# A transformer block pair on one core: one product shared by two projection tiles, and a later chunk's transposes placed in an earlier wait

## The chip, the cores and the metric

The kernel runs on one core of one Trainium2 chip. The metric is device time in microseconds (us). A time is the median of three runs. A profile is one further execution, with every instruction's start and length. Below, PE is TensorE (matmuls; its weight loads are PEld), DVE is VectorE, ACT is ScalarE, POOL is GpSimd and SP is SyncE, whose queue issues nearly all transfers.

## The reference

Two layers, each of multi-query attention (16 heads of width 28, one key and one value head) and a gated feed-forward, on 2048 rows of width 448, with the same weights in both layers.

```python
def _A_ref(x, wq, wk, wv, wo):
    q = (x @ wq).reshape(B, S, H, Dh).transpose(0, 2, 1, 3)
    k = x @ wk
    v = x @ wv
    scores = jnp.einsum("bhqd,bkd->bhqk", q, k) * (Dh ** -0.5)
    o = jnp.einsum("bhqk,bkd->bhqd", _softmax(scores), v)
    return o.transpose(0, 2, 1, 3).reshape(B, S, H * Dh) @ wo

def _B_ref(x, w_gate, w_up, w_down):
    return (_silu(x @ w_gate) * (x @ w_up)) @ w_down

x = x + _A_ref(_layernorm(x), ...)
x = x + _B_ref(_layernorm(x), ...)
x = x + _A_ref(_layernorm(x), ...)
x = x + _B_ref(_layernorm(x), ...)
```

Everything is float32. The kernel splits each operand of a product into a rounded high part and a remainder (h and l, float32r) and adds three products: high by high, high by low, low by high.

## The kernel before

The 2048 rows are cut into four chunks of 512. The order in which the code is written is the order on each engine; no scheduler moves instructions. An engine works through its own instructions in that order and waits where one of them has to.

**Projections.** For each chunk there are four tiles of 128 columns, 16 products per layer. They are called q0 to q15 here, in the order of `Attention.order`; q0 to q3 belong to chunk 0, q12 to q15 to chunk 3. A tile holds 112 columns of queries and 16 of keys or values. `project()` runs one tile: first what `plan[n, 0]` names, then the transposes of a chunk that is due (`turned`, by `flip`), then the product (`q`), then what `plan[n, 1]` and `when[n]` name. `q` takes a PSUM bank, runs `product_T`, and then evacuates: ScalarE casts the queries (L538), ScalarE copies the tile to a buffer named `stage` (L539), SP issues its store to DRAM (`qd`, L540, and for two tiles of a chunk the keys to `kt`, L543), and for the other two VectorE transposes the value columns (L546) and GpSimd places them (L549). In layer 0 there are three `stage` buffers, in layer 1 two, so there a copy waits until the stores of the tile before last have landed.

**The inner dimension** is 448: three slices of 128 and one of 64. For the last slice `xh[:, 3]` holds the high part in its lower 64 partitions and the remainder in its upper 64, and the weights stand in both halves. So one product of 128 rows gives two of the three terms. The third takes one more product, with the weights' low part `wl`, whose upper half adds the low part times the remainder, a term that the other slices leave out. That makes 11 products a tile:

```python
        for k in range(3):
            seq += [(a_h[k], xh[:, k, :]), (a_h[k], xl[:, k, :]), (a_l[k], xh[:, k, :])]
        seq += [(a_h[3], xh[:, 3, :]), (a_l[3], xh[:, 3, :])]
```

**The feed-forward** already works by half rows: products of 64 rows on partitions 0 to 63 and 64 to 127 are issued alternately by `side_by_side` (L332) into two banks and run at the same time. For it a third tile `xd` holds the last slice's high part in partitions 64 to 127.

**Chunks of layer 1.** Chunks 0 to 2 are transposed by VectorE into DRAM at the end of the feed-forward of layer 0, loaded back by SP (`load`, L934 to L937, into the buffers `qstack`), and split into `xh` and `xl` by `halved`: ScalarE casts (L292, L296), VectorE subtracts (L293, L302). Chunk 3 is transposed by TensorE (`flip`, L248, 16 transposes) from the normalised tile `xn`; ScalarE casts from PSUM (L254, L258) and VectorE subtracts (L255, L264). For chunk 2 the load is issued after q4 (`plan[4, 1]`), and the splitting, called `parts`, stands ahead of q7 (`plan[7, 0]`). SP has one queue: after the load of chunk 2 come a load of keys (`wrk`, L398), four of queries (`qraw`, L421) and then the stores of q5. Each transfer of the queue also takes one of eight completion counters (DMAHW0 to DMAHW7), in turn, and waits until the transfer that had it before has landed.

Of the kernel before, what the change touches and what calls it, by code (L numbers as in the profile page):

```python
# [9 lines left out]
F32R = mybir.dt.float32r  # L10
# [5 lines left out]
P = 128  # L16
# [7 lines left out]
NC = S // 512  # L24
# [31 lines left out]
def forward(  # L56
# [14 lines left out]
    nc = tc.nc  # L71
# [13 lines left out]
    xpool = ctx.enter_context(tc.tile_pool(name="xpool", bufs=1))  # L85
# [4 lines left out]
    wide = [ALL]  # L90
# [20 lines left out]
    def bank(cands, hold=False):  # L111

        for _ in cands:
            turn[cands] = (turn.get(cands, -1) + 1) % len(cands)
            b = cands[turn[cands]]
            if b not in live:
                if hold:
                    live.add(b)
                return b, banks[b]
        raise AssertionError("no bank")  # L120
# [82 lines left out]
    def xtile(pool, again=None):  # L203

        return (
            pool.tile([P, 4, 512], F32R, name="xh"),
            pool.tile([P, 3, 512], F32R, name="xl"),
            again,
        )
# [33 lines left out]
    def flip(got, tiles, ks=range(4), place=None):  # L243

        for k in ks:
            pt = place if place is not None else bank(wide[-1])[1]
            for t in range(4):
                nc.tensor.transpose(pt[:, P * t : P * t + P], got["x"][:, t, P * k : P * k + P], ident)  # L248
            flipped(tiles, k, pt, nc.vector.tensor_copy if place is not None else nc.scalar.copy)
# [16 lines left out]
    def turn_tile(got, tb, t):  # L266

        nc.vector.transpose(tb[:, :, 32 * t : 32 * t + 32], got["x"][:, t, 0:D].rearrange("p (b w) -> p b w", w=32))
# [7 lines left out]
    def natural(po, squares):  # L276

        if not squares:
            return po
        return po.rearrange("p (g t w) -> p t g w", g=4, w=32)  # L280

    def in_order(a, squares):

        return a.rearrange("p (t g w) -> p t g w", g=4, w=32) if squares else a
# [19 lines left out]
    def product_T(po, a_h, a_l, tiles):  # L304

        xh, xl = tiles[:2]
        seq = []
# [3 lines that stand above are left out]
        for i, (a, b) in enumerate(seq):  # L311
            nc.tensor.matmul(po, a, b, start=(i == 0), stop=(i == len(seq) - 1))  # L312
# [14 lines left out]
    def side_by_side(lower, upper):  # L327

        assert len(lower) == len(upper)
        for two in zip(lower, upper):  # L330
            for po, (a, b), start, stop in two:
                nc.tensor.matmul(po, a, b, start=start, stop=stop, skip_group_check=True)  # L332
# [10 lines left out]
    class Attention:  # L343
# [152 lines left out]
        def project(self):  # L496

            c, m = self.order[self.seen]
            for f in self.plan.get((self.seen, 0), ()):
                f()  # L500
            late = self.layer == 0 and self.seen == 3
            turned = [self.order[n][0] for n in (self.seen, self.seen + 1) if n % 4 == 0 and n < len(self.order)]
            for o in turned if not late else ():
                self.turned(o)
            self.q(c, m)
            for o in turned if late else ():
                self.turned(o)
            for f in self.plan.get((self.seen, 1), []) + self.when.pop(self.seen, []):
                f()
            self.seen += 1  # L510

        def turned(self, c):
            if c in self.norms:
                flip(self.norms.pop(c), self.X[c])

        def q(self, c, m):
            cs = slice(512 * c, 512 * c + 512)
            sq = c in self.squares
            held, po = bank((3, 4, 5) if self.seen > len(self.order) - 4 else wide[-1], True)
            ms = slice(P * m, P * m + P)  # L520
            wh, wl = self.w
            product_T(po, [wh[:, k, ms] for k in range(4)], [wl[:, k, ms] for k in range(4)], self.X[c])
            if not full and self.seen in (6, 10, 14):
                self.maxima(self.seen // 4 - 1)()
            live.remove(held)
            if c not in self.qd:
                self.qd[c] = dram.tile([D, 512], F32, name=f"qd{self.layer}_{c}")
            if self.layer and c == NC - 1:
                if "xn" not in self.spare:
                    self.spare["xn"] = pers.tile([P, 4, 512], F32, name="xn")  # L530
                raw = self.spare["xn"][:, self.seen % 4, :]
            else:
                raw = self.pool.tile([P, 512], F32, name="stage")
            if not full:
                if self.seen % 2 == 0:
                    self.two = wpool.tile([P, 2, 512], F32R, tag="wgh", name="q2", bufs=FG + 1)
                self.hi[c, m] = self.two[0:112, self.seen % 2, :]
                nc.scalar.copy(in_order(self.hi[c, m], sq), natural(po[0:112, :], sq))  # L538
            nc.scalar.copy(in_order(raw, sq), natural(po, sq))  # L539
            nc.sync.dma_start(self.qd[c][112 * m : 112 * m + 112, :], raw[0:112, :])  # L540
            d0, n = 16 * (m % 2), 12 if m % 2 else 16
            if m > 1:
                nc.sync.dma_start(self.kt[c][d0 : d0 + n, :], raw[112 : 112 + n, :])  # L543
                return
            vt = wpool.tile([P, 512], F32R, tag="wgl", name="vt", bufs=FG + 1).bitcast(F32)[96:128, :]
            nc.vector.transpose(vt, po[96:128, :])  # L546
            vt = vt.rearrange("p (u t d) -> p u t d" if sq else "p (t u d) -> p u t d", t=4, u=4)
            for u in range(4):
                nc.gpsimd.tensor_copy(  # L549
                    vsb[32 * u : 32 * u + 32, 4 * c : 4 * c + 4, d0 : d0 + n], vt[:, u, :, 16 : 16 + n]  # L550
                )
# [285 lines left out]
    class FeedForward:  # L837
# [61 lines left out]
        def hand_over(self, c):  # L899

            a = self.nxt
            fs, got = norm_steps(c, twice=c == NC - 1)
            for f in fs[:5]:
                f()
            a.pool = self.stage

            if c == NC - 1:

                def ready():
                    for f in fs[5:]:  # L910
                        f()
                    a.norms[c] = got

                a.X[c] = xtile(self.xbp)
                a.plan[5, 1] = [ready]
                return
            to = dram.tile([D, 512], F32, name=f"xt1_{c}")
            raw = [q.bitcast(F32)[:, z, :] for q in qts[1:] for z in range(2)]

            def turn():  # L920
                for f in fs[5:]:
                    f()
                pool = (xpool, self.x1p, self.xbp)
                tb = pool[min(c + 1, 2)].tile([P, 4, 512], F32R, name="xh").bitcast(F32)
                tb = tb.rearrange("p a (b n) -> p (a b) n", n=P)[:, 0 : D // 32, :]
                for t in range(4):
                    turn_tile(got, tb, t)
                send(tb, to)
                a.X[c] = xtile(pool[c])
                if c < 2:  # L930
                    load()

            def load():
                nc.sync.dma_start(qts[1].bitcast(F32), to[0:256, :].rearrange("(k p) n -> p k n", p=P))  # L934
                nc.sync.dma_start(raw[2], to[256:384, :])
                for half in (slice(0, 64), slice(64, 128)):
                    nc.sync.dma_start(raw[3][half, :], to[384:448, :])  # L937

            def parts():
                halved(a.X[c], raw, range(4), nc.scalar.copy, nc.vector.tensor_tensor)  # L940

            self.soon.append([1, turn])
            if c == 2:
                a.plan[4, 1] = [load]
                a.plan[7, 0] = [parts]
                return
            self.soon.append([3, parts])
            self.soon.append([4 - c, lambda: [a.project() for _ in range(2 - c)]])
# [128 lines left out]
    xb = ExitStack()  # L1077
    at = Attention(0)
    at.pool = xb.enter_context(tc.tile_pool(name="stage_", bufs=3))
    xbp = xb.enter_context(tc.tile_pool(name="xb0", bufs=3))  # L1080
# [16 lines left out]
    for c in (1, 2, 3):  # L1097
        load_x(c, nc.sync)
    at.below(nc.sync)
    at.X = {c: xtile(xpool if c == 0 else xbp) for c in range(NC)}  # L1100
    at.turned(0)
    nc.gpsimd.memset(vsb, 0.0)
    nc.gpsimd.memset(vsb[:, :, DH : DH + 1], 1.0)
# [15 lines left out]
    for layer in range(2):  # L1119
# [3 lines left out]
        xb = ExitStack()  # L1123
        at.scores(ff, xb)
        ff.rest(xb)
        at = ff.nxt
# [28 lines left out]
```

## Time and profile before

| | us |
|---|---|
| median of three runs | 1962.71 (1962.13 to 1963.45) |
| the profiled execution | 1962.25 |
| its span, first instruction to last | 1960.4 |
| projections of layer 0, from q0 to the first score | 12.0 to 63.7 |
| attention of layer 0 | 63.7 to 556 |
| feed-forward of layer 0 | 556 to 971 |
| projections of layer 1 among the last units of the feed-forward | 971.9 to 1032.9 |
| attention, then feed-forward of layer 1 | 1032.9 to 1526, to 1960.4 |

A row of a timeline gives the start, the length, the engine, the source line, the operation, output and inputs by name, the shape, and a count where equal rows were merged; in brackets stands the idle time before it and what ended it. Matmuls are pipelined, so one of 0.39 us length is followed by the next long before that time is over: what one costs is read from start to start. A product of 128 rows has "128\*128" and one of half rows "64\*128" in its row. On the SP queue (SPq) a row is the issue of a transfer, not the transfer.

### The profile page before, as it was taken

What the parts mean: (1) busy time and instruction counts of PE and PEld (TensorE: products, weight loads), DVE (VectorE), ACT (ScalarE), POOL (GpSimd) and SP (SyncE); (2) the same over time, 40 slices, a digit from 0 to 9 for tenths busy, and PEclk for the clock granted to TensorE, in tenths of its full rate; (3) what the DMA queues carried; (4) which work ended last, traced back from release to release, by engine and by line L of the source; (5) the groups of instructions that cost most, each with busy time, mean ns of one, the idle gap of its engine ahead of it and who ended that gap; (6) DMA issues with size and microseconds to landing.
All of it is one profiled execution on the core that took longest, in us unless ns stands there. A gap on an engine that the chain in (4) does not pass through costs nothing.

```text
span 1960.4 us, 44004 instructions
## 1 busy us (share of the span) xinstructions
PE 1943.3 (99%) x18469; PEld 1325.5 (68%) x18469; DVE 968.3 (49%) x1638; ACT 1264.1 (64%) x1888; POOL 553.6 (28%) x593
## 2 busy tenths in 40 slices
PE   9999999999999999999999999999999999999998
PEld 7544545445468999999974445454454799988886
DVE  6656575665743223223666565657656433223223
ACT  4899898998943333333349998989989333333332
POOL 4213123132214333333341221121231332323320
PEclk9999999999999999999999999999999999999999
DMA  5111011121130011110251110110211200011102
GB/s 166 55 36 29 21 40 40 29 53 43 26 87 20 17 32 32 32 29 19 67 156 34 37 30 22 50 28 24 67 40 32 71 28 21 17 32 32 32 2 77
DMA packets 100643, 83.61 MB, mean 43 GB/s; under 512 B 25080, under 2 KB 81656, under 8 KB 100440
## 3 DMA queue, kind: packets, MB, share of 16 engines
q1 hardware_dynamic: 98888, 79.55, 14.7%
q8 instruction: 145, 2.38, 0.5%
q10 hardware_dynamic: 1552, 1.20, 0.2%
q14 instruction: 58, 0.48, 0.1%
HBM read 57.38 MB, written 21.50 MB: 40 GB/s over the span
## 4 chain that ended last, share of the span: by engine, by line
PE 87%; ACT 9%; DMA 1%; DVE 1%; issue 1%; POOL 0%; SPq 0%; ACTq 0%; POOLq 0%; DVEq 0%
PE bank L332 40%; PE bank L688 20%; PE bank L633 14%; ACT pt L655 6%; PE three L633 5%; PE bank L312 4%; ACT pair L656 2%; PE three L612 2%; PE bank L612 1%; PE three L621 0%; PE bank L438 0%; DMA kt<-stage 0%; DMA xd<-xh 0%; DMA wr<-in_A_wq_dram 0%; DVE vt L546 0%
## 5 line engine op out<-in xcount | busy, mean ns | idle before, releaser
L655 ACT ACTIVATE pt<-three 128x1536 f32<-128x1536 f32 x512 | 723.0, 1484 | 52.9 <-PE three L633 52.9
L688 PE MATMUL bank<-pt,vsb 128*32 128x512 f32 x3072 | 490.8, 599 | 0.0
L688 PE MATMUL bank<-pair,vsb 128*32 128x512 f32 x1024 | 487.5, 598 | 0.6 <-ACT pair L656 0.6
L633 PE MATMUL bank<-qstack,keys 32*128 32x512 f32 x1536 | 473.1, 425 | 0.0
L332 PE MATMUL bank<-xh,wgh 64*128 64x512 f32 x1728 | 450.7, 389 | 0.0
L633 PE MATMUL three<-qstack,keys 32*128 32x512 f32 x4608 | 428.7, 408 | 0.5 <-ACT stage L539 0.3
L633 PEld LDWEIGHTS bank<-qstack,keys 32*128 32x128 f32 x1536 | 243.5, 183 | 250.0 <-issue 124.9
L654 DVE COPY pair<-bank 128x512 f32<-128x512 f32 x512 | 354.0, 691 | 95.2 <-PE bank L633 57.4
L332 PE MATMUL bank<-xh,wgl 64*128 64x512 f32 x1404 | 371.7, 391 | 0.0
L332 PE MATMUL bank<-xl,wgh 64*128 64x512 f32 x1296 | 338.1, 390 | 0.0
L332 PE MATMUL bank<-wdh,h 64*128 64x448 f32 x1792 | 334.3, 364 | 1.1 <-ACT h L1008 0.8
L1007 DVE TENSOR_TENSOR sg<-bank,sg 128x512 f32<-128x512 f32 x112 | 77.4, 691 | 502.5 <-ACT sg L1006 500.3
L656 ACT ACTIVATE pair<-pair 128x1024 f32<-128x1024 f32 x256 | 281.5, 1100 | 0.0
L332 PEld LDWEIGHTS bank<-xh,wgh 64*128 64x128 f32 x1728 | 266.3, 185 | 16.7 <-issue 1.3
L633 PEld LDWEIGHTS three<-qstack,keys 32*128 32x128 f32 x4608 | 261.5, 183 | 13.9 <-DVE xres L604 1.5
L885 POOL TENSOR_TENSOR xres<-stage,xres 128x448 f32<-128x448 f32 x108 | 127.3, 1197 | 502.5 <-ACT stage L884 502.3
L688 PEld LDWEIGHTS bank<-pt,vsb 128*32 128x32 f32 x3072 | 101.9, 109 | 246.0 <-issue 153.1
L332 PEld LDWEIGHTS bank<-wdh,h 64*128 64x128 f32 x1792 | 247.5, 184 | 14.8 <-issue 2.0
L697 DVE TENSOR_TENSOR o<-bank,o 128x512 f32<-128x512 f32 x224 | 154.9, 691 | 203.8 <-PE bank L688 203.8
L339 ACT COPY seen<-bank 128x1 f32<-128x1 f32 x664 | 81.9, 163 | 254.3 <-PE bank L332 251.2
L332 PEld LDWEIGHTS bank<-xh,wgl 64*128 64x128 f32 x1404 | 219.2, 184 | 13.8
L332 PE MATMUL bank<-wdl,h 64*128 64x448 f32 x896 | 222.2, 367 | 0.0
(145 smaller groups left out, 2095.7 us busy)
## 6 DMA issues: line engine op xcount, KB each, us to landing
o<-rd SPq DMA_DIRECT2D x32, 256.0 KB
qraw<-qd SPq DMA_DIRECT2D x128, 56.0 KB
qd<-stage SPq DMA_DIRECT2D x28, 224.0 KB
wdr<-in_B_w_down_dram SPq DMA_DIRECT2D x28, 224.0 KB
xt<-tb SPq DMA_DIRECT2D x24, 224.0 KB
wr<-in_B_w_gate_dram SPq DMA_DIRECT2D x28, 192.0 KB
wr<-in_B_w_up_dram SPq DMA_DIRECT2D x28, 192.0 KB
xn<-xt SPq DMA_DIRECT2D x6, 768.0 KB
```

Source lines behind the costliest of these rows:

```text
L312: nc.tensor.matmul(po, a, b, start=(i == 0), stop=(i == len(seq) - 1))
L332: nc.tensor.matmul(po, a, b, start=start, stop=stop, skip_group_check=True)
L339: nc.scalar.copy(seen[:, i : i + 1], po[:, 0:1])
L612: nc.tensor.matmul(po[:, 0:D], a[:, g, P * t : P * t + P], b[:, g, :], start=False, stop=(g == NG - 1 and z == 2), skip_group_check=True,)
L633: nc.tensor.matmul(three[:, j, :] if j < 3 else one, k[js, kp, ks], q[js, part, :], start=(z == 0), stop=(z == 2), tile_position=(32 * j, 0),)
L654: copies.append(nc.vector.tensor_copy(pt1, one))
L655: es.append(nc.scalar.activation(pt, threes[y], AF.Exp, scale=SCALE))
L656: es.append(nc.scalar.activation(pair, pair, AF.Exp, scale=SCALE))
L688: nc.tensor.matmul(to[32 * j : 32 * j + 32, :], vsb[:, n % NT, :], pts[n][j], start=(y == 0), stop=(y == 1), skip_group_check=True,)
L697: f = nc.vector.tensor_tensor(accs[i][:, 0, :], to, accs[i][:, 0, :], ALU.add)
L885: nc.gpsimd.tensor_tensor(r, s, r, ALU.add)
L1007: nc.vector.tensor_tensor(in_order(sg, sq), natural(pg[1], sq), in_order(sg, sq), ALU.mult)
```

## The change

Two tiles of a chunk share the eleventh product. The first of a pair (q0, q2, ...) runs ten products of 128 rows, and then two of 64 rows side by side: on the lower half its own third term of the last slice, and on the upper half the third term of the second tile, which opens the second tile's bank; it reads `xd`. The second tile then runs its ten products into that bank. This holds for all chunks but chunk 0 of layer 0, which has no `xd`. For it the chunks get an `xd` tile, and the last slice is cast in two halves (L299 and L300 in `halved`, L261 and L262 in `flipped`, lines of the changed kernel), where it was one cast. In layer 1 the transposes of chunk 3 move from q11 to q8, and chunk 2's `parts` from ahead of q7 to ahead of q8.

```diff
@@ project
             turned = [self.order[n][0] for n in (self.seen, self.seen + 1) if n % 4 == 0 and n < len(self.order)]
+            if self.layer and self.seen == 8:
+                turned = [NC - 1]
             for o in turned if not late else ():
                 self.turned(o)
@@ Attention
+        def pair(self, po):
+
+            c, m = self.order[self.seen]
+            xh, xl, xd = self.X[c]
+            wh, wl = self.w
+            ms = slice(P * m, P * m + P)
+            a_h, a_l = [wh[:, k, ms] for k in range(4)], [wl[:, k, ms] for k in range(4)]
+            seq = []
+            for k in range(3):
+                seq += [(a_h[k], xh[:, k, :]), (a_h[k], xl[:, k, :]), (a_l[k], xh[:, k, :])]
+            seq.append((a_h[3], xh[:, 3, :]))
+            if self.seen % 2:
+                for i, (a, b) in enumerate(seq):
+                    nc.tensor.matmul(po, a, b, start=False, stop=(i == 9), skip_group_check=True)
+                return
+            for i, (a, b) in enumerate(seq):
+                nc.tensor.matmul(po, a, b, start=(i == 0), stop=False, skip_group_check=True)
+            m2 = self.order[self.seen + 1][1]
+            self.next = self.own_bank(1)
+            side_by_side(
+                [(po, (wl[0:64, 3, ms], xh[0:64, 3, :]), False, True)],
+                [(self.next[1], (wl[64:128, 3, P * m2 : P * m2 + P], xd[64:128, :]), True, False)],
+            )
+
+        def own_bank(self, ahead):
+
+            return bank((3, 4, 5) if self.seen + ahead > len(self.order) - 4 else wide[-1], True)
@@ q
-            held, po = bank((3, 4, 5) if self.seen > len(self.order) - 4 else wide[-1], True)
...
-            product_T(po, [wh[:, k, ms] for k in range(4)], [wl[:, k, ms] for k in range(4)], self.X[c])
+            if self.X[c][2] is None:
+                held, po = self.own_bank(0)
+                product_T(po, [wh[:, k, ms] for k in range(4)], [wl[:, k, ms] for k in range(4)], self.X[c])
+            else:
+                held, po = self.next if self.seen % 2 else self.own_bank(0)
+                self.pair(po)
@@ hand_over (c == NC - 1)
-                a.X[c] = xtile(self.xbp)
+                a.X[c] = xtile(self.xbp, self.xd[c])
@@ hand_over (turn)
-                a.X[c] = xtile(pool[c])
+                a.X[c] = xtile(pool[c], self.xd[c])
@@ hand_over (c == 2)
-                a.plan[7, 0] = [parts]
+                a.plan[8, 0] = [parts]
@@ forward
-    at.X = {c: xtile(xpool if c == 0 else xbp) for c in range(NC)}
+    xdp = xb.enter_context(tc.tile_pool(name="xd_", bufs=1))
+    at.X = {c: xtile(xbp, xdp.tile([P, 512], F32R, name=f"xd_{c}")) for c in range(1, NC)}
+    at.X[0] = xtile(xpool)
```

TensorE's order in layer 0, at the border between q4 and q5 (the first pair), before. The bank's name ends in a number of its own; `wh` and `wl` are the weights' two parts:

```order
L312 MATMUL bank_83<-xl,wh 128x512
L312 MATMUL bank_83<-xh,wl 128x512
L312 MATMUL bank_83<-xh,wh 128x512
L312 MATMUL bank_83<-xh,wl 128x512
L312 MATMUL bank_84<-xh,wh 128x512
L312 MATMUL bank_84<-xl,wh 128x512
L312 MATMUL bank_84<-xh,wl 128x512
```

The same border in the changed kernel:

```order
L530 MATMUL bank_83<-xl,wh 128x512
L530 MATMUL bank_83<-xh,wl 128x512
L530 MATMUL bank_83<-xh,wh 128x512
L332 MATMUL bank_83<-xh,wl 128x512
L332 MATMUL bank_84<-xd_221,wl 128x512
L527 MATMUL bank_84<-xh,wh 128x512
L527 MATMUL bank_84<-xl,wh 128x512
L527 MATMUL bank_84<-xh,wl 128x512
```

The last product of q4 has become two of half rows (L332), the second into q5's bank, and at q5's end the same product is gone.

ScalarE's order in layer 1 at q7 and the splitting of chunk 2, before. `stage_11645` is q6's buffer, `stage_11677` q7's; the brackets name what an instruction waits for:

```order
L539 COPY stage_11645<-bank2_6437 128x512 [waits DMAHW1_49,DMAHW0_49,Activation_49]
L292 CAST xh_11492<-qstack1_101 128x512 [waits DMAHW2_49]
L292 CAST xh_11492<-qstack1_101 128x512
L292 CAST xh_11492<-qstack2_102 128x512 [waits DMAHW3_49]
L296 CAST xh_11492<-qstack2_102 128x512 [waits DMAHW5_49,DMAHW4_49]
L538 CAST q2_11646<-bank3_6438 112x512 [waits PE_49]
L539 COPY stage_11677<-bank3_6438 128x512 [waits DMAHW4_49,DMAHW3_49,Activation_49]
```

And in the changed kernel, where `stage_11658` is q6's and `stage_11681` q7's:

```order
L573 COPY stage_11658<-bank2_6447 128x512 [waits DMAHW1_49,DMAHW0_49,Activation_49]
L572 CAST q2_11659<-bank3_6448 112x512 [waits PE_49]
L573 COPY stage_11681<-bank3_6448 128x512 [waits DMAHW4_49,DMAHW3_49,Activation_49]
L292 CAST xh_11505<-qstack1_101 128x512 [waits DMAHW2_49]
L292 CAST xh_11505<-qstack1_101 128x512
L292 CAST xh_11505<-qstack2_102 128x512
L299 CAST xd2_6632<-qstack2_102 64x512 [waits DMAHW5_49]
L300 CAST xh_11505<-qstack2_102 64x512
L254 CAST xh_11575<-bank4_6449 128x512 [waits DMAHW6_49,DVE_49,PE_49]
```

q7's cast and copy now stand ahead of chunk 2's casts, the last cast is two, and behind them come the casts of chunk 3 out of PSUM. VectorE's order in the changed kernel at the same place (before, the L293 and L302 rows stood between the two value transposes, then L546):

```order
L580 STREAM_TRANSPOSE vt_11663<-bank2_6447 32x512 [waits Activation_49]
L580 STREAM_TRANSPOSE vt_11685<-bank3_6448 32x512 [waits PE_49,Activation_49]
L293 TENSOR_TENSOR xl_11506<-qstack1_101,xh_11505 128x512 [waits DMAHW2_49,Activation_49]
L293 TENSOR_TENSOR xl_11506<-qstack1_101,xh_11505 128x512 [waits Activation_49]
L293 TENSOR_TENSOR xl_11506<-qstack2_102,xh_11505 128x512 [waits DMAHW3_49,Activation_49]
L302 TENSOR_TENSOR xh_11505<-qstack2_102,xd2_6632 64x512 [waits DMAHW5_49,Activation_49]
L255 TENSOR_TENSOR xl_11576<-bank4_6449,xh_11575 128x512 [waits Activation_49]
```

q7's value transpose (`vt_11685`) waits for q7's copy on ScalarE, and the subtractions of chunk 2 stand behind it. SP's order of transfers is the same in both kernels.

## The prediction

> **What bounds the kernel now.** I read the page's busy table first, then the chain of waits, then the timelines of the engines around the two stretches of projections.
>
> ```profile
> span 1960.4 us, 44004 instructions
> PE 1943.3 (99%) x18469; PEld 1325.5 (68%) x18469; DVE 968.3 (49%) x1638; ACT 1264.1 (64%) x1888; POOL 553.6 (28%) x593
> PE 87%; ACT 9%; DMA 1%; DVE 1%; issue 1%; POOL 0%; SPq 0%; ACTq 0%; POOLq 0%; DVEq 0%
> ```
>
> TensorE is busy for 99% of the span and carries 87% of the chain, so a slot taken from it in a stretch without holes is a gain, and a slot added is a loss. The change touches only the projections: layer 0 up to 63.7 us and layer 1 from 971.9 to 1032.8 us. Windows of both:
>
> ```profile
> 22.00:64.00 42.00, 41.44 (x204) 33.34 (x206) 30.81 (x61) 19.51 (x38) 22.44 (x56) 1.00 0.37 108
> 971.00:1033.00 62.00, 59.59 (x307) 46.89 (x308) 38.73 (x76) 29.38 (x63) 28.05 (x54) 0.97 0.51 145
> ```
>
> The columns are length, then busy time of PE, PEld, DVE, ACT and POOL, the granted clock and DMA. Layer 0 has no hole worth the name, layer 1 loses 2.4 us to holes and has a granted clock below 1. I write q0 to q15 for the sixteen projections of a layer in their order. The first instructions of q9 and q10 in layer 0, the first score matmul behind layer 0, and the first of q0 in layer 1:
>
> ```profile
> 39.28 0.39 PE L312 MATMUL bank<-xh,wh 128*128 128x512 f32 x1
> 41.77 0.39 PE L312 MATMUL bank<-xh,wh 128*128 128x512 f32 x1
> 63.71 0.50 PE L633 MATMUL bank<-qstack,keys 32*128 32x512 f32 x1
> 971.90 0.50 PE L312 MATMUL bank<-xh,wh 128*128 128x512 f32 x1
> ```
>
> Eleven matmuls lie between the first two starts: 2.49 / 11 = 0.226 us a slot.
>
> **The shared product.** A pair of projections had 22 slots and gets 21: ten, one in which two 64-row products run side by side, ten. Taken alone that is -0.226 us. But it sets TensorE from 128 rows to 64 and back within the pair. The trace has both turns, where projections of layer 1 stand next to half-row products of the feed-forward:
>
> ```profile
> 976.81 0.39 PE L312 MATMUL bank<-xh,wl 128*128 128x512 f32 x1
> 977.13 0.49 PE L332 MATMUL bank<-xh,wgh 64*128 64x512 f32 x2
> 977.47 0.39 PE L332 MATMUL bank<-xl,wgh 64*128 64x512 f32 x2
> 984.35 0.36 PE L332 MATMUL bank<-wdh,h 64*128 64x448 f32 x2
> 984.64 0.50 PE L312 MATMUL bank<-xh,wh 128*128 128x512 f32 x1
> 984.98 0.40 PE L312 MATMUL bank<-xl,wh 128*128 128x512 f32 x1
> ```
>
> To 64 rows: 977.47 - 976.81 = 0.66 us for what should take two slots, 0.45, so +0.21. Back to 128: 0.63 us for a 448-column slot (448/512 of 0.226 = 0.20) and a full one, so +0.20. (The x2 rows are two products started together, so side by side works.) A pair costs -0.23 + 0.21 + 0.20 = **+0.18 us**. Bounds: -0.23 if a lone half-row slot hides both turns, +0.3 if it adds a drain of its own; I take the measured turns, as they are the same change of row count. The Trainium skill, "TensorEngine Tiling", section "Key Properties", says that changing the tiling mode, unlike changing the tile, drains TensorE; the rows above agree, with 0.2 us. By the promise of up to 2x in its "Overview" alone a pair would gain 0.23.
>
> Six pairs in layer 0, with TensorE full: +1.1. Of layer 1's eight, the first (q0, q1) delays what follows it, +0.2; q2 to q7 end in a hole, so cost nothing unless it closes; the last four count, +0.7.
>
> Copies: where a chunk's last slice was one cast on ScalarE it is two now, of half the partitions. Layer 0 covers that (ScalarE is busy 19.5 of 42 us). In layer 1 it delays what VectorE does after q2 by 0 to 0.5 us: +0.25.
>
> **The hole in layer 1.** Between q7 and q8 TensorE waits for chunk 2:
>
> ```profile
> 1003.99 0.39 PE L312 MATMUL bank<-xh,wl 128*128 128x512 f32 x1
> 1006.10 0.50 PE L312 MATMUL bank<-xh,wh 128*128 128x512 f32 x1 [1.72 <-ACT xh L292]
> 1006.82 0.50 PE L312 MATMUL bank<-xl,wh 128*128 128x512 f32 x1 [0.22 <-DVE xl L293]
> 1007.50:1011.00 3.50, 3.50 (x10) 2.74 (x9) 1.25 (x2) 1.08 (x2) 1.34 (x3) 0.52 0.49 163
> ```
>
> The last row, a window, shows that after the hole the clock is granted by half for 3.5 us, which costs 3.5 x 0.48 = 1.7 us. The change moves chunk 3's 16 transposes from before q11 into this hole:
>
> ```profile
> 1016.77 1.91 PE L248 MATMUL bank<-ident,xn 128*128 128x128 f32 x16
> 1018.43 0.48 PE L312 MATMUL bank<-xh,wh 128*128 128x512 f32 x1
> ```
>
> That takes 1.66 us off the path. But it also moves chunk 2's casts from ahead of q7's evacuation to behind it, on ScalarE (L292, L296 against L538, L539) and on VectorE (L293, L302 against q7's L546). What they now stand behind:
>
> ```profile
> 1002.57 0.59 ACT L539 COPY stage<-bank 128x512 f32<-128x512 f32 x1 [0.53 <-DMA kt<-stage]
> 1005.43 1.88 ACT L292 CAST xh<-qstack 128x512 fp32r<-128x512 f32 x3 [2.27 <-DMA qstack<-xt]
> 1007.48 0.62 ACT L296 CAST xh<-qstack 128x512 fp32r<-128x512 f32 x1 [0.17 <-DMA qstack<-xt]
> 1008.00 0.58 ACT L538 CAST q<-bank 112x512 fp32r<-112x512 f32 x1
> 1011.52 0.58 ACT L539 COPY stage<-bank 128x512 f32<-128x512 f32 x1 [2.94 <-DMA kt<-stage]
> 1006.08 1.98 DVE L293 TENSOR_TENSOR xl<-qstack,xh 128x512 fp32r<-128x512 f32 x3
> 1012.14 0.72 DVE L546 STREAM_TRANSPOSE vt<-bank 32x512 f32<-32x512 f32 x1 [3.32 <-ACT stage L539]
> 1001.10 0.39 SPq L934 DMA_DIRECT2D qstack<-xt  x1
> 1006.73 0.31 SPq L540 DMA_DIRECT2D qd<-stage  x1
> 1007.09 0.42 SPq L543 DMA_DIRECT2D kt<-stage  x1
> ```
>
> q7's L539 at 1011.52 fills a stage buffer. There are two, so it takes q5's, and waits until q5's stores, issued on SP at 1006.73 and 1007.09 behind the load of chunk 2, have landed. SP's order is not changed, so that moment stays. Before, this wait of 2.94 us hurt nobody: the casts were done. Now they queue behind it. ScalarE casts at 1011.52 + 0.5 (as from L296 to L538) = 1012.0 in place of 1005.43; VectorE does q7's transpose at 1012.14 and the first subtraction at 1012.89 in place of 1006.08. So q8's second matmul starts near 1013.6 in place of 1006.82: **+6.8 us**. The moved steps issue no transfer, and GpSimd's order stays too. The transposes fill 1.7 us of a hole that is now about 8 us long.
>
> Behind that point two stalls shrink. q13 waited at a bank that q11's evacuation gave back late, again behind a store:
>
> ```profile
> 1023.33 0.39 PE L312 MATMUL bank<-xh,wl 128*128 128x512 f32 x1
> 1024.18 0.50 PE L312 MATMUL bank<-xh,wh 128*128 128x512 f32 x1 [0.47 <-DVE vt L546]
> 1032.85 0.49 PE L633 MATMUL bank<-qstack,keys 32*128 32x512 f32 x1
> ```
>
> That is 0.85 - 0.23 = 0.6 us; with all of q8 to q11 later than the loads in their way I take it as gone (0 to 0.6). The half clock after the hole stays: the hole is longer than the one that brought it. TensorE restarts somewhere inside such a stretch, so the loss is 0.4 to 2.1 us, I take 1.2 where it was 1.7: -0.5. The last row, the first score matmul, would then stand near 1037.5.
>
> **Sum** against the profiled execution (1962.25 us, its span 1960.4): +1.1 (layer 0) +0.2 +0.25 (ahead of the hole) +6.8 (casts) -1.66 (transposes) -0.6 (bank) -0.5 (clock) +0.7 (four pairs) = +6.3. That execution lies 0.46 below the median of 1962.71, so the sum gives 1968.5 from its own time and 1969.0 from the median; I say **1968.8 us**.
>
> **Rivals.** *The evacuation does not wait.* If q5's stores had landed by the time q7 ends, the casts would start with the load, at 1005.43, and the transposes would close the hole: +1.1 +0.2 +0.25 -1.66 -0.6 +0.7 -1.7 (clock kept) = -1.7, **1961.0**. It decides below a landing near 1005.5. For it: q4's store, just ahead of the load, held the copy of 1002.57 back for 0.53 us only. Against: q5's stores are issued at 1006.73, after that point. Chance 0.05.
>
> *The stores land sooner,* say 2 us after issue, near 1009, since fewer transfers compete: 2.4 less, **1966.4**. Nothing on SP moved, so 0.1.
>
> *The turns are hidden:* 0.41 less for each of the eleven pairs that count, **1964.3**. The weight loads of 977.13 and 984.64 did not start early, so 0.07. "TensorE: Matmul & The Clock Gate" in the Trainium skill, section "The mechanism", has loads pulled ahead of running matmuls when row groups do not conflict; a 128-row load conflicts with both halves, and no run here shows otherwise.
>
> *Clock and bank stall both go the bad way:* +0.9 and +0.6, **1970.3**. Chance 0.1.
>
> *The transposes do not reach the hole,* because chunk 3 is not normalised in time or their four banks are not free: +1.66, **1970.5**. Against it stands GpSimd's last step on that chunk, over by 1003.3:
>
> ```profile
> 1001.78 1.51 POOL L232 COPY xn<-xn 128x64 f32<-128x64 f32 x4 [0.61 <-DVE xn L230]
> ```
>
> Chance 0.03.
>
> **Chances.** My forecast has the remaining 0.65. About 0.2% (3.9 us) is what a measurement of this kernel can tell from no change. Faster by more than that needs the first rival and hidden turns together, or a cause that I do not see: 0.03. Within it lie the rest of the first rival, hidden turns, and half of the sooner landing, 0.16 with the edge of my forecast. Slower: 0.81. The range reaches from just above the hidden turns to beyond the two bad cases: 1964.6 to 1971.2.
>
> **What would show it.** On ScalarE q7's stage copy should begin near 1012 to 1014 (all later by the 1.5 us ahead of it), with a wait for a store before it, and L292 right behind it; on TensorE 16 transposes after q7, then about 6 us idle, then q8 at half clock for a while. Half-row rows in the pairs should start 0.3 us after the slot before, and the slot behind them as late again. I am wrong if L292 still starts when the load lands, if the hole is under 3 us, or if layer 0's projections end earlier than 63.7 us.

## The result and the profile after

| | us |
|---|---|
| median, changed kernel (six runs) | 1970.5 (1969.05 to 1973.07) |
| median, kernel before, on the same chip (six runs) | 1962.61 (1961.65 to 1963.45) |
| ratio | 1.0041, 95% interval 1.0031 to 1.0051 |
| profiled execution of the changed kernel | 1969.38 |

The change costs 7.9 us by the medians, and 7.1 us between the two profiled executions (1969.38 against 1962.25). The six times of the changed kernel lie in two groups, three near 1969.2 and three from 1971.6 up; why is open.

The busy table and the chain of the changed kernel, then windows of layer 0's and layer 1's projections and of the stretch of half clock (length, busy time of PE, PEld, DVE, ACT and POOL, granted clock, DMA):

```profile
span 1967.6 us, 44011 instructions
PE 1945.0 (99%) x18469; PEld 1325.5 (67%) x18469; DVE 968.5 (49%) x1638; ACT 1267.9 (64%) x1895; POOL 555.2 (28%) x593
PE 87%; ACT 10%; DMA 1%; issue 1%; DVE 1%; POOL 0%; SPq 0%; ACTq 0%; POOLq 0%; DVEq 0%
```

```profile
22.00:64.00 42.00, 41.41 (x199) 31.53 (x198) 30.13 (x59) 21.00 (x41) 22.74 (x57) 1.00 0.37 106
971.00:1040.00 69.00, 62.38 (x320) 46.50 (x318) 39.58 (x78) 31.16 (x65) 28.24 (x55) 0.95 0.46 131
1012.50:1019.30 6.80, 4.42 (x10) 3.10 (x10) 5.03 (x8) 5.68 (x11) 5.79 (x8) 0.50 0.36 106
```

The totals say almost nothing: TensorE is busy for 99% of either span. The second window does. Layer 1's projections leave TensorE idle for 69.0 - 62.4 = 6.6 us, where before it was 2.4, and the third shows the clock at half for 6.8 us where it was 3.5.

What fills that hole is on ScalarE's timeline of the changed kernel (start, length, line, operation, and in brackets the idle time before it and what ended it). L573 is the stage copy, L572 the queries' cast, L292 the first casts of chunk 2:

```profile
1004.74 0.59 ACT L573 COPY stage<-bank 128x512 f32<-128x512 f32 x1 [0.35 <-DMA kt<-stage]
1006.55 0.59 ACT L572 CAST q<-bank 112x512 fp32r<-112x512 f32 x1 [1.22 <-PE bank L527]
1013.55 0.59 ACT L573 COPY stage<-bank 128x512 f32<-128x512 f32 x1 [6.42 <-DMA kt<-stage]
1014.04 1.66 ACT L292 CAST xh<-qstack 128x512 fp32r<-128x512 f32 x3
```

q7's cast is done at 1007.1, and ScalarE then stands for 6.42 us before q7's stage copy, until a store has landed. Chunk 2's casts come right behind the copy. Which store that is, SP's queue shows: L968 begins the load of chunk 2, L574 and L577 are q5's stores.

```profile
1003.28 0.39 SPq L968 DMA_DIRECT2D qstack<-xt  x1
1008.61 0.31 SPq L574 DMA_DIRECT2D qd<-stage  x1
1008.96 0.42 SPq L577 DMA_DIRECT2D kt<-stage  x1
```

They go out 5.3 and 5.7 us behind the load (before: 5.6 and 6.0), and the copy starts 4.6 us after the second. VectorE and TensorE at the same place:

```profile
1014.17 0.72 DVE L580 STREAM_TRANSPOSE vt<-bank 32x512 f32<-32x512 f32 x1 [6.00 <-ACT stage L573]
1014.93 1.95 DVE L293 TENSOR_TENSOR xl<-qstack,xh 128x512 fp32r<-128x512 f32 x3
```

```profile
1006.35 1.91 PE L248 MATMUL bank<-ident,xn 128*128 128x128 f32 x16
1014.71 0.79 PE L530 MATMUL bank<-xh,wh 128*128 128x512 f32 x1 [6.45 <-ACT xh L292]
1015.67 0.80 PE L530 MATMUL bank<-xl,wh 128*128 128x512 f32 x1 [0.17 <-DVE xl L293]
1016.27 0.63 PE L530 MATMUL bank<-xh,wl 128*128 128x512 f32 x1
1039.98 0.50 PE L667 MATMUL bank<-qstack,keys 32*128 32x512 f32 x1
```

The 16 transposes do run in the hole, right behind q7, and still 6.45 us of it are left; q8 then runs at half clock (0.63 us a row instead of 0.39). The last row is the first score of layer 1.

The shared product in layer 0, in the pair q8, q9, which has no stall in it: its first row, the rows around its two turns, and the first row of q10. The last row is the first score:

```profile
39.68 0.39 PE L530 MATMUL bank<-xh,wh 128*128 128x512 f32 x1
...
41.73 0.39 PE L530 MATMUL bank<-xh,wh 128*128 128x512 f32 x1
42.05 0.50 PE L332 MATMUL bank<-xh,wl 64*128 64x512 f32 x1
42.05 0.50 PE L332 MATMUL bank<-xd,wl 64*128 64x512 f32 x1
42.48 0.50 PE L527 MATMUL bank<-xh,wh 128*128 128x512 f32 x1
42.81 0.40 PE L527 MATMUL bank<-xl,wh 128*128 128x512 f32 x1
...
44.88 0.39 PE L530 MATMUL bank<-xh,wh 128*128 128x512 f32 x1
...
64.66 0.49 PE L667 MATMUL bank<-qstack,keys 32*128 32x512 f32 x1
```

The two half-row products do start together. From the last full slot to them are 0.32 us, from them to the next full one 0.43, and from that to the one behind it 0.33, where plain slots are 0.226 apart. The pair takes 44.88 - 39.68 = 5.20 us, where 22 plain slots of 0.226 take 4.98. (The rows at 39.28 and 41.77 before, called q9 and q10 in the prediction, are the starts of q8 and q9; the slot time read from them is the same.)

### The profile page after: what moved, and what is told of

It is laid out like the page before. It is cut to its first block, busy times and chain, and to the rows that moved or that the text cites. A ratio compares the mean times of both kernels' runs of the same rounds, so it can differ in the third digit from the quotient of the medians.

```text
span 1967.6 us, 44011 instructions
## 1 busy us (share of the span) xinstructions
PE 1945.0 (99%) x18469; PEld 1325.5 (67%) x18469; DVE 968.5 (49%) x1638; ACT 1267.9 (64%) x1895; POOL 555.2 (28%) x593
## 4 chain that ended last, share of the span: by engine, by line
PE 87%; ACT 10%; DMA 1%; issue 1%; DVE 1%; POOL 0%; SPq 0%; ACTq 0%; POOLq 0%; DVEq 0%
PE bank L332 40%; PE bank L722 20%; PE bank L667 14%; ACT pt L689 6%; PE three L667 5%; ACT pair L690 2%; PE three L646 2%; PE bank L312 2%; PE bank L530 1%; PE bank L527 1%; PE bank L646 1%; PE three L655 0%; PE bank L438 0%; PE bank L248 0%; DMA qstack<-xt 0%
## 5 line engine op out<-in xcount | busy, mean ns | idle before, releaser
L332 PE MATMUL bank<-xh,wgh 64*128 64x512 f32 x1728 | 447.5, 389 | 0.1
L332 PE MATMUL bank<-xh,wgl 64*128 64x512 f32 x1404 | 369.5, 390 | 0.0
L332 PE MATMUL bank<-xl,wgh 64*128 64x512 f32 x1296 | 335.7, 389 | 0.0
L332 PE MATMUL bank<-wdh,h 64*128 64x448 f32 x1792 | 333.5, 363 | 1.1 <-ACT h L1042 0.8
L332 PEld LDWEIGHTS bank<-xh,wgh 64*128 64x128 f32 x1728 | 265.5, 184 | 16.1 <-issue 1.3
L332 PEld LDWEIGHTS bank<-wdh,h 64*128 64x128 f32 x1792 | 247.3, 184 | 13.7 <-issue 2.0
L332 PEld LDWEIGHTS bank<-xh,wgl 64*128 64x128 f32 x1404 | 218.6, 184 | 13.2
L332 PE MATMUL bank<-wdl,h 64*128 64x448 f32 x896 | 220.6, 366 | 0.0
```

## The experiments

The table puts the nine experiments beside the two kernels; each ratio is to the kernel before on the same chip (medians of 1962.51 to 1962.79). The last three columns are from each kernel's profile, in us after the issue of chunk 2's load: when ScalarE casts chunk 2, when it makes q11's stage copy, and when the first score of layer 1 starts. The load itself goes out 937.4 to 938.8 us behind the first score of layer 0 in all of them, and from the first score of layer 1 to the end are 927.4 to 928.5 us: what differs lies between the last column's two ends, for the most part. The first score of layer 0 itself starts between 63.7 and 66.4 us; the two latest, pairs alone (66.4) and transposes alone (66.0), are late already ahead of the first pair.

| kernel | median us | ratio to before, 95% interval | casts | q11's copy | first score |
|---|---|---|---|---|---|
| before | 1962.71 | | 4.33 | 21.63 | 31.76 |
| changed | 1970.50 | 1.0041 (1.0031 to 1.0051) | 10.76 | 26.00 | 36.70 |
| casts back | 1967.74 | 1.0028 (1.0017 to 1.0039) | 3.90 | 22.15 | 34.24 |
| pairs alone | 1964.00 | 1.0008 (0.9999 to 1.0017) | 3.84 | 21.53 | 31.71 |
| transposes alone | 1965.28 | 1.0013 (1.0004 to 1.0022) | 4.46 | 21.64 | 34.27 |
| another buffer for q7 | 1966.11 | 1.0016 (1.0007 to 1.0025) | 4.24 | 21.57 | 33.66 |
| no pairs | 1967.70 | 1.0027 (1.0017 to 1.0036) | 10.65 | 25.00 | 35.34 |
| transposes, own buffers | 1958.96 | 0.9983 (0.9974 to 0.9992) | 3.90 | 17.39 | 27.76 |
| change, own buffers | 1962.82 | 0.9999 (0.9990 to 1.0008) | 4.24 | 18.43 | 29.14 |
| before, own buffers | 1961.80 | 0.9992 (0.9983 to 1.0001) | 4.01 | 20.57 | 31.12 |
| q9's stores elsewhere | 1962.02 | 0.9995 (0.9986 to 1.0004) | 4.24 | 18.43 | 29.14 |

### Casts back: chunk 2's split ahead of q7's evacuation again

```diff
-                a.plan[8, 0] = [parts]
+                a.plan[7, 0] = [parts]
```

> The changed kernel, but chunk 2's casts and subtractions stand ahead of q7's evacuation again; pairs and the earlier transposes stay. Theory (the 6 us come from the casts queued behind q7's stage copy, which waits for q5's stores): L292 starts when the load lands, the hole on TensorE is about 2 us and mostly filled by the transposes, time 1961 to 1963.5. Rival A (the pairs' turns are the main cost): 1966 or more. Rival B (the transposes at q8 are what holds q8 back): 1968 or more.

Measured 1967.74: 2.8 us of the 7.9 came back, not six to nine. The casts do start with the load (3.90 us after it), and the hole ahead of q8 is gone. A new one is there, ahead of q13's product, on TensorE's and ScalarE's timelines of this kernel:

```profile
1009.01 0.49 PE L530 MATMUL bank<-xl,wh 128*128 128x512 f32 x1 [0.45 <-DVE xl L293]
1026.94 0.50 PE L332 MATMUL bank<-xd,wl 64*128 64x512 f32 x1 [3.59 <-DVE vt L580]
```

```profile
1019.94 0.59 ACT L573 COPY stage<-bank 128x512 f32<-128x512 f32 x1 [0.96 <-DMA kt<-stage]
1025.49 0.58 ACT L573 COPY stage<-bank 128x512 f32<-128x512 f32 x1 [4.21 <-DMA kt<-stage]
```

q13's bank is freed by q11's value transpose on VectorE, which stands behind q11's stage copy, and that copy (1025.49) waited 4.21 us for a store of q9. So the theory that the order of the casts explains all of the loss fell. The time lies where rival A was put, but its cause is this hole, and the next run speaks against the turns as the main cost.

### Pairs alone: neither the casts nor the transposes moved

```diff
-            if self.layer and self.seen == 8:
-                turned = [NC - 1]
...
-                a.plan[8, 0] = [parts]
+                a.plan[7, 0] = [parts]
```

> The kernel before with the pairs and their xd tiles alone; casts and transposes where they were. Theory: a pair costs +0.2 us where TensorE is full (a slot saved, two turns of 0.2 us paid), eleven pairs count, so 1964 to 1965.5. Rival A: 1966 or more. Rival C (the turns are hidden, a pair saves its slot): 1959.5 to 1961.5.

1964.0, at the lower end of what was expected: by the medians the shared product, with the split casts that it needs, costs some 1.2 us when nothing else is changed, with an interval that still holds no change. Behind the load the four pairs cost nothing here (31.71 us to the first score, before 31.76).

### Transposes alone: the kernel before, chunk 3 transposed at q8

```diff
+            if self.layer and self.seen == 8:
+                turned = [NC - 1]
```

> The kernel before with chunk 3's transposes ahead of q8 alone; casts of chunk 2 stay ahead of q7's evacuation, no pairs. Theory: 1.7 us of transposes leave the path, the bank stall of 0.6 us may go, and the clock may stay whole (0 to 1.7): 1958.5 to 1961. Rival B: 1962.5 or more.

A miss on the wrong side: 1965.28, slower than before. The transposes fill the hole at q8, as meant, and the hole at q13 takes back more than that:

```profile
1006.80 1.91 PE L248 MATMUL bank<-ident,xn 128*128 128x128 f32 x16
1009.58 0.50 PE L312 MATMUL bank<-xl,wh 128*128 128x512 f32 x1 [0.23 <-DVE xl L293]
1026.81 0.80 PE L312 MATMUL bank<-xh,wh 128*128 128x512 f32 x1 [3.53 <-DVE vt L548]
```

```profile
1025.36 0.59 ACT L541 COPY stage<-bank 128x512 f32<-128x512 f32 x1 [3.94 <-DMA kt<-stage]
```

```profile
1025.40:1032.20 6.80, 5.39 (x13) 4.23 (x14) 1.45 (x2) 1.81 (x4) 4.72 (x12) 0.50 0.35 109
```

TensorE comes to q13 sooner, q11's copy doesn't (21.64 us after the load, before 21.63), and from inside the hole on the clock is at half for 6.8 us, as the window shows, where before it was 3.4 (at q8). The time is in rival B's range, but not by its mechanism: q8 starts on time, and q13 is what waits.

### Another buffer for q7: the changed kernel's order without the wait

```diff
+            elif self.layer and self.seen == 7:
+                raw = halves("raw7").bitcast(F32)[:, 0, :]
             else:
                 raw = self.pool.tile([P, 512], F32, name="stage")
```

`halves` is a pair of tiles that the kernel has already and does not use at this point.

> The changed kernel, but q7's copy goes to a buffer of its own, so that it waits for no store; the order of all engines stays as changed. Theory (the wait for the buffer is the cause, not the order by itself): q7's copy follows its cast at once, L292 starts when the load lands, time 1961 to 1963.5, as with the casts put back. Rival D (the order itself costs, casts behind an evacuation): 1966 or more.

ScalarE's and TensorE's rows:

```profile
1006.99 0.59 ACT L575 COPY raw<-bank 128x512 f32<-128x512 f32 x1
1007.47 1.84 ACT L292 CAST xh<-qstack 128x512 fp32r<-128x512 f32 x3
1024.80 0.59 ACT L575 COPY stage<-bank 128x512 f32<-128x512 f32 x1 [3.02 <-DMA kt<-stage]
1026.26 0.50 PE L332 MATMUL bank<-xd,wl 64*128 64x512 f32 x1 [2.40 <-DVE vt L582]
```

The casts start 4.24 us after the load, so the wait of q7's copy was what held them, with the order on ScalarE unchanged. The time fell to 1966.11 only: a wait of 2.40 us (a gap of 2.90 from start to start) stands ahead of q13, and q11's copy is again 21.57 us behind the load. That is rival D's range, but the order is not what costs: the last experiment below keeps it and takes 1962.02. The prediction's first rival, an evacuation that does not wait, was given 1961.0; this run is the nearest to it, and it is 5 us worse.

### No pairs: the changed kernel with the plain product everywhere

```diff
-            if self.X[c][2] is None:
+            if True:
```

> The changed kernel without the shared products (each tile runs its eleven products of 128 rows); casts behind q7's evacuation, early transposes and split casts stay. Theory: the pairs that count go, 1 to 2 us less than the changed kernel: 1968.5 to 1969.5; the hole ahead of q8 stays at 6 to 7 us. Rival A (the turns are the main cost): 1966 or less.

1967.70, somewhat below what was expected; the hole at q8 stays (TensorE waits 6.80 us there). By the medians the pairs account for 2.8 of the 7.9 us, between the two profiled executions for 1.8 (1969.38 - 1967.56), and against the lower group of the changed kernel's times for 1.4.

### Transposes with buffers of their own

The claim was now that early transposes are worth something only if q11's copy comes sooner too. Here q7, q8, q10 and q11 get buffers of their own, on top of the transposes alone; q9's copy then is the only one behind q6 that uses a `stage` buffer.

```diff
+            elif self.layer and self.seen in (7, 8, 10, 11):
+                if self.seen in (7, 10):
+                    self.own = halves("rawown").bitcast(F32)
+                raw = self.own[:, int(self.seen in (8, 11)), :]
```

> The kernel before with early transposes, and buffers of their own for the copies of q7, q8, q10 and q11 of layer 1 (no pairs). Second theory (early transposes only move the wait: q13's bank waits for q11's copy, which waits for q9's stores to leave the second stage buffer): the gap of 3.9 us ahead of q13 goes, and with it the half clock behind it, 1958.5 to 1960.5. Rival E (the gap comes from somewhere else on VectorE or GpSimd): the gap stays, 1964 or more.

1958.96, faster than both kernels (0.9983, at most 0.9992). From the load to the first score it takes 27.76 us where before it took 31.76. TensorE's only wait at chunk 2, and the window from the load to the first score:

```profile
1004.89 1.91 PE L248 MATMUL bank<-ident,xn 128*128 128x128 f32 x16
1007.48 0.50 PE L312 MATMUL bank<-xl,wh 128*128 128x512 f32 x1 [0.45 <-DVE xl L293]
```

```profile
1001.80:1029.60 27.80, 27.35 (x131) 21.95 (x129) 18.70 (x33) 14.38 (x27) 18.23 (x39) 1.00 0.60 174
```

No hole at q13, and the granted clock is 1.00 throughout.

### The same buffers under the whole change, and under the kernel before

> The changed kernel, all of it, with those four buffers of their own. Second theory: neither q8 nor q13 waits for a store, so only the pairs and split casts are left as a cost: 1960 to 1962, 1 to 2 above the kernel before with early transposes and the same buffers. Rival E: 1965 or more.

> The kernel before with the four buffers alone. Second theory: only the short stall ahead of q13 (0.6 us) goes, the hole ahead of q8 stays: 1961.5 to 1962.7. If it comes near 1959, the buffers and not the transposes are what the other kernels with buffers gain.

The whole change with these buffers takes 1962.82, 0.8 us above what was expected and 7.7 below the change without them. Against 1958.96 the kernels differ in the pairs with their split casts, and in chunk 2's casts, which stand behind q7's evacuation here and ahead of it there; no run takes these apart. In the profiles 0.76 us of the 3.86 lie ahead of layer 0's first score, 0.76 between q0 and the load, 1.38 from the load to the first score of layer 1, and 0.99 behind that, where neither edit does anything. The kernel before gains 1.0 us by the medians from the buffers (1961.80), with an interval that still holds no change: its hole at q8 waits for the load, not for a buffer. So buffers alone give little, early transposes alone lose 2.5 us, and both together gain 3.8.

### q9's stores on another queue

What sets the 21.57 us there? SP's and GpSimd's timelines of the kernel with another buffer for q7 suggested an answer. L136 on GpSimd is the split of the keys loaded before (`wrk`), L398 on SP the next load into the same buffer, and L576 and L579 at 1018.97 and 1019.45 are q9's stores:

```profile
1017.02 1.27 POOL L136 TENSOR_TENSOR keys<-wrk,keys 128x512 fp32r<-128x512 f32 x1
```

```profile
1018.32 0.55 SPq L398 DMA_DIRECT2D wrk<-kt  x1
1018.97 0.43 SPq L576 DMA_DIRECT2D qd<-stage  x1
1019.45 0.42 SPq L579 DMA_DIRECT2D kt<-stage  x1
```

The load goes out when GpSimd is done with the buffer (1017.02 + 1.27 = 1018.29), and q9's stores, whose data were there at 1016.2, stand behind it. Of the 2.8 us that they wait, 0.7 are the load's wait for GpSimd; the rest is what SP still has to issue ahead of them, loads of queries, q8's stores and this load.

```diff
-            nc.sync.dma_start(self.qd[c][112 * m : 112 * m + 112, :], raw[0:112, :])
+            out = nc.scalar if self.layer and self.seen == 9 else nc.sync
+            out.dma_start(self.qd[c][112 * m : 112 * m + 112, :], raw[0:112, :])
...
-                nc.sync.dma_start(self.kt[c][d0 : d0 + n, :], raw[112 : 112 + n, :])
+                out.dma_start(self.kt[c][d0 : d0 + n, :], raw[112 : 112 + n, :])
```

> The changed kernel with a buffer of its own for q7, as before, and q9's two stores (qd, kt) issued on ScalarE's queue instead of SP's. If it is SP's queue that decides (q9's stores stand there behind the load of keys, which goes out only when GpSimd has split the keys before it: 1018.32, with the stores at 1018.97 and 1019.45, while q9's copy was over at 1016.2), the stores go out near 1016.5, 2.5 us earlier, q11's copy begins near 1022.3 instead of 1024.80, TensorE's wait of 2.90 us ahead of q13 falls to under 0.6 and brings no half clock: 1961.5 to 1963. Rival: the transfers' own traffic decides when the buffer comes free, whatever queue they go out on: q11's copy stays behind 1024, the wait behind 2 us, and the time at 1965.5 to 1966.5.

1962.02, inside the range of the queue's theory and far from the rival's. On ScalarE's timeline (ACTq is the issue from its queue) the stores leave 2.9 us sooner and q11's copy has no wait at all:

```profile
1015.43 0.59 ACT L575 COPY stage<-bank 128x512 f32<-128x512 f32 x1
1016.05 0.38 ACTq L577 DMA_DIRECT2D qd<-stage  x1
1016.47 0.52 ACTq L580 DMA_DIRECT2D kt<-stage  x1
...
1021.54 0.59 ACT L575 COPY stage<-bank 128x512 f32<-128x512 f32 x1
```

The place of q9's two stores in a queue was thus worth 1966.11 - 1962.02 = 4.1 us by the medians: the hole of 2.9 and what the half clock behind it costs. How much of that the wait for GpSimd alone makes is not shown, since the stores left the whole queue.

This holds for the kernel with another buffer for q7. With casts back the hole at q13 comes another way, as its ScalarE and SP show:

```profile
1013.32 0.59 ACT L573 COPY stage<-bank 128x512 f32<-128x512 f32 x1 [2.34 <-DMA kt<-stage]
1017.88 0.61 ACT L573 COPY stage<-bank 128x512 f32<-128x512 f32 x1
```

```profile
1019.04 0.42 SPq L574 DMA_DIRECT2D qd<-stage  x1
```

q9's copy (1017.88) is itself late there: it stands on ScalarE behind chunk 3's casts and q7's copy (1013.32), which waited for q5's stores. Its store goes out 0.55 us after the copy ends, so SP's queue explains little. With the transposes alone it is the same, with 0.86 us. What the three kernels have in common is the ring of two stage buffers, not the queue.

## Why the prediction was right, and where it would have failed

It gave 1968.8 (1964.6 to 1971.2) and slower; measured were 1970.5 and slower. Step by step, with the profiled executions:

**The wait.** Right in mechanism and in size. The copy's wait for q5's stores was carried over from before, where it was harmless, and the casts queued behind it. Against the load the casts come 10.76 - 4.33 = 6.4 us later (said: 6.6), and q8's second matmul 12.39 - 5.72 = 6.7 us later (said: 6.8). Both rivals with times near the measured one, 1970.3 and 1970.5, are not what happened: the transposes ran in the hole, and the stall at q13 is gone. The buffer experiment shows the cause: without that one wait the casts start with the load.

**Behind the hole.** Said were -1.66 for the transposes, -0.6 for the bank stall, -0.5 for the clock and +0.7 for four pairs, together -2.06; from q8's second matmul to the first score the changed kernel takes 24.31 us and the kernel before 26.04, that is -1.73. The transposes left the path and the stall at q13 is gone, as said; the term that was off most is the clock, which did not get better: from the second matmul on it is at half for 3.6 us (1015.67 to 1019.3), where before it was 3.4. That is inside the bounds that were given for it.

**Ahead of the hole.** Two terms were mis-sized. Layer 0 ends 0.95 us later (64.66 against 63.71; said: 1.1). Of that 0.2 lies ahead of the first pair (q4 starts at 25.64 against 25.43), so the six pairs cost 0.74, though one without a stall costs 0.22 (said: 0.18): where the turn stands beside the transposes of a chunk these take 0.16 and 0.23 us less than before (1.67 against 1.83, 1.67 against 1.90). The half-row rows start 0.32 us after the slot before (said: 0.3), the slot behind them 0.43 later (said: 0.3). Of loads of 128 rows the prediction says that no run shows them pulled ahead; that is so at the turns, where the load of 984.64 starts with its own product, but between products of 128 rows the load for the product of 976.81 runs from 976.59, beside the product before it. The load goes out 2.18 us later, 1.23 beyond layer 0 (said: +0.2 and +0.25). From q0 to the load it takes 29.20 to 29.22 us in the four profiles with the plain casts and products, 29.76 without pairs and 29.97 to 29.99 with them: the split casts cost 0.55 where 0.25 were put down, and the pairs 0.2, as said. The other 0.45 lie between the first score and q0, where the change does nothing; 908.18 us before, 908.5 to 908.8 in every other profile, so it is the profile of before that was short there.

**The sum.** 0.95 + 1.23 + 4.94 = 7.1 in place of 6.3. By the medians it was 7.9; the three lower times alone lie 6.5 above the median of before, the three upper ones 9 to 10.5.

**The step that would have failed** is the first rival's: "If q5's stores had landed by the time q7 ends, the casts would start with the load, at 1005.43, and the transposes would close the hole", with 1961.0. It takes each hole as a loss of its own: of the stall at q13 the prediction says "I take it as gone (0 to 0.6)". With the hole at q8 closed, in three kernels that keep the two stage buffers for q8 to q11 (casts back, transposes alone, another buffer for q7), that stall grew to 2.9 to 4.1 us, and the clock's half stretch moved there. In the changed kernel itself it stayed hidden behind the larger hole.

What stays open: the two groups of times of the changed kernel, and why the pairs cost 1.2 us alone, 1.4 to 2.8 inside the change and up to 3.9 with own buffers (the first and the last with the split casts, the last with the casts' place too), where eleven pairs that count, at 0.18, make 2.0. For the two groups more half clock would fit: the three lower runs have mean granted clocks of 0.998, 0.997 and 0.998, the three upper ones 0.997, 0.997 and 0.995, and 0.0013 of 1970 us is 2.6 of the 3.1 us between the groups' means. This is not shown, since no upper run has a profile and 0.001 of the span is 2 us. But the profile of the transposes alone has a granted clock of 0.50 from 11.7 to 18.3 us, where the kernel before has 1.00, and its time of 1967.69 is 2.4 above the median of its own kernel, 1965.28.

## What to carry to other kernels

Before moving work behind an instruction, look at the wait that this instruction already has, even where it hurts nobody: what queues behind it inherits it. Work moved into a hole pays only up to the next place where the same resource ends the wait: here two stage buffers were behind both holes, so follow the buffer through the whole stretch (copy, store, queue of the store, landing, next copy) before counting the hole as won. And look at what stands in the queue ahead of a store that gives back a scarce buffer: here 2.8 us of other transfers and their waits stood there, and a hole of 2.9 us closed when the stores left that queue.

## What the runs showed of the hardware

**A short hole can bring half a clock, and the stretch has two lengths.** Before, a hole of 1.72 us of waiting (1004.4 to 1006.1) was followed by 3.41 us at half clock; the half-clock stretches at the holes of layer 1 in the profiles here are 3.41 us long or twice that, and a long one can begin inside the hole. The changed kernel, with 6.45 us of waiting, and the transposes alone, with 3.53, got the long one; the kernels with casts back (3.59) and with another buffer (2.40) got the short one, so the length of the hole does not decide alone. The Trainium skill, "TensorE: Matmul & The Clock Gate", section "What's actually happening", gives a free-running window of 3413 ns, which agrees with the lengths; it has the half rate set in after at least one idle window, and here a wait of half that length was enough.

**A lone slot of 64 rows between products of 128 rows** makes three steps of 0.32, 0.43 and 0.33 us where plain slots are 0.226 apart, 0.40 us more together, so each turn of row count costs 0.2 us even around a single slot. A product shared by two tiles in this way loses 0.22 us a pair (5.20 against 4.98).

**Where a transfer is issued from can matter more than its issue.** The Trainium skill, "DMA: Bandwidth & Descriptors", section "Issuing engines are not separate DMA queues", says that issuing on several engines saves only the time on the sequencer, usually small. With q9's stores the saving was 2.9 us: they no longer stood behind what SP had to issue first, of which 0.7 us was a load's wait for GpSimd.
